# Attention's results stored and reloaded by head, and block-diagonal queries copied once per head

## The chip, the cores and the metric

The kernel runs on one core of a Trainium2 chip. Its engines are TensorE (PE, with its weight loads PEld), VectorE (DVE), ScalarE (ACT), GpSimd (POOL) and SyncE (SP, which here issues every DMA). The metric is device time in microseconds (us), the median of several executions.

## The reference

An attention and two feed-forward layers, one behind the other, all in float32:

```python
# q, k, v: (4 batches, 8 heads, 576 positions, 64)
scores = (q @ k^T) / sqrt(64)
scores = where(pos_i // 64 >= pos_j // 64, scores, -1e9)   # causal by blocks of 64
attn = exp(scores - max);  attn = attn / (sum(attn) + 1e-9)
x = (attn @ v) as (2304 tokens, 512)
h = x @ w_in;  x = (h * clip(h + 3, 0, 6) / 6) @ w_out       # w_in 512x2048, w_out 2048x512
h = x @ w_in2; x = (h * tanh(log1p(exp(h)))) @ w_out2
```

## The kernel before

**Attention** handles 16 pairs of heads, p0 to p15 (4 batches, 4 pairs in each). A value is split in a high and a low part, so that a product takes three matmuls. Queries and keys of a pair come in as `q` and `k` (128 partitions: 64 of each head, 576 positions), and POOL splits them into `qs` and `ks` (`split`, L443 for the high part, L303 for the low one). A pair has three rounds of scores: AC and D, in which each head has its own rows of PE (L526), and BE, in which both heads share a matmul (L495): its stationary operand is block-diagonal, with head 0's queries in one corner, head 1's in the other, and zeros beside them. For p0 POOL copies them into these tiles; for the other pairs DMAs do it, in `last_queries`: four DMAs of 32 KB into `qb` and two into `qe`. The exponentials (ACT, tiles `p..`) are transposed on PE (L555), split again into `z`, and multiplied by the values (L619) into one bank `o`. That is copied out to `x` and stored to DRAM as `x1d[pair of the batch, part, head and dim, token]`, with four DMAs of 64 rows a pair (`attn_v`); the two parts are the 64 upper and 64 lower rows of `x`, which are added later. The reciprocals of the sums go to `rsd` with three DMAs (`sums`).

**First layer.** Tokens run in blocks j (512 columns, the last 256) of four tiles k. `tokens1(j, k)` loads the two parts into `xr` and `xs` (128 rows each), the reciprocals into `xn` (two loads of 64 rows), adds (L934) and scales (L938) on POOL or DVE, and splits the result into the seven `X` tiles (ACT the high part, L303 the low one). `xr` has two buffers, `xs` and `xn` one. PE then runs `h` and `y` (L792 to L794) over 16 slices of weights, which are loaded as `raw` (512 KB each) and rebuilt by ACT, POOL and DVE. **Second layer:** the same with fewer products by sums of blocks; its weights are prepared during the first (`unit2`).

**What sets the order.** Nothing is ordered by hand: `Schedule` takes each operation with its engine, its estimated cost and the names it reads and writes, and writes one sequence per engine. An engine then runs its sequence strictly in order, and a DMA at the head of SP's sequence that waits for its data holds all that stand behind it. The sequence of PE mixes the end of attention with the start of the first layer: the first `h` matmuls stand among the last L619.

Of the kernel before, what the change touches and what calls it, by code (L numbers as in the profile page):

```python
# [10 lines left out]
F32R = mybir.dt.float32r  # L11
# [7 lines left out]
P = 128  # L19
# [210 lines left out]
def f32(ap):  # L230
    return ap.bitcast(F32)
# [7 lines left out]
def fused_kernel(ctx: ExitStack, tc: tile.TileContext, qT, kT, vv, w1, w2, outT):  # L239
# [80 lines left out]
    for n in range(2):  # L320
        for t in "qk":
            at[t, n] = aq.tile([P, S], F32, tag=t, name=f"{t}{n}")
            at[t + "s", n] = aq.tile([P, 2, S], F32R, tag=t + "s", name=f"{t}s{n}")
        at["qb", n] = aq.tile([P, 2, 2, P], F32R, tag="qb", name=f"qb{n}")
        at["qe", n] = aq.tile([P, 2, P], F32R, tag="qe", name=f"qe{n}")
        at["s", n] = ps_s.tile([P, 1024], F32, tag="s", name=f"s{n}")
        at["v", n] = a2.tile([P, 5, P], F32, tag="v", name=f"v{n}")
        at["vb", n] = ap.tile([P, 5, 2, 2, 64], F32R, tag=f"vh{n}", name=f"vh{n}")
        at["z", n] = ap.tile([P, 2, 2, 5 * ZC], F32R, tag=f"t{n}", name=f"z{n}")
        at["su", n] = sm.tile([P, NB], F32, tag="su", name=f"su{n}", bufs=2)  # L330
        at["rs", n] = sm.tile([NB, P], F32, tag="rs", name=f"rs{n}", bufs=2)
        for h in range(2):
            at["x", h, n] = a2.tile([P, S], F32, tag=f"x{h}", name=f"x{h}_{n}")
# [9 lines left out]
    for u in ("AC", "D", "B"):  # L343
# [9 lines left out]
    EARLY_TILES = (  # L353
        [(t, n, j) for t in "qk" for n in range(2) for j in range(2)]
        + [(t, n, i, j) for t in ("qs", "ks") for n in range(2) for i in range(2) for j in range(2)]
        + [("qb", n, j, i) for n in range(2) for j in range(2) for i in range(3)] + [("mask",), ("ones",), ("hold",)]
        + [("s", n) for n in range(2)])
    LATE_TILES = (
        [("v", n) for n in range(2)] + [("vb", n, t) for n in range(2) for t in range(2)]
# [48 lines left out]

    def last_queries(p):
        n = p % 2  # L410
        if p == 0:
            for j in range(2):
                r = slice(64 * j, 64 * j + 64)
                by = lambda t: t.rearrange("p t (n d) -> p t n d", d=64)
                for i, w, dst, src in (
                        (1, 256, at["qb", 0][r, :, :, r], by(at["qs", 0][r, :, P:2 * P])),
                        (0, 128, at["qe", 0][r, :, r], at["qs", 0][r, :, 512:576])):
                    plan.add(
                        one("POOL", "POOL_ONE", w), [("qs", 0, t, 1 - i) for t in range(2)],
                        [("qb", 0, j, m) for m in range(i, 2 * i + 1)],  # L420
                        lambda e, dst=dst, src=src: nc.gpsimd.tensor_scalar(
                            dst, f32(src), 1.0, 1.0, op0=ALU.mult, op1=ALU.mult), after=hold)
            return
        for j in range(2):
            r = slice(64 * j, 64 * j + 64)
            for t in range(2):
                dma(160, [("qs", n, t, 0)], [("qb", n, j, 1 + t)], f32(at["qb", n][r, t, :, r]),
                    f32(at["qs", n][r, t, P:2 * P]).rearrange("p (n d) -> p n d", d=64), land=LAND)
            dma(160, [("qs", n, t, 1) for t in range(2)], [("qb", n, j, 0)],
                f32(at["qe", n][r, :, r]), f32(at["qs", n][r, :, 512:576]), land=LAND)  # L430

    def split(p, t):
        n = p % 2
# [33 lines left out]
    def scores(g):  # L467
# [19 lines left out]

        products = ((0, 0), (0, 1), (1, 0))
        if u == "BE":
            stationary = at["qe", n], at["qb", n][:, :, 0], at["qb", n][:, :, 1]  # L490

            def run(e):
                for k, (x, y) in enumerate(products):
                    for i, a, z, o in BOTH:
                        nc.tensor.matmul(  # L495
                            sc[:, a:z], stationary[i][:, x, :], ks[:, y, a - o:z - o], start=k == 0 and a in (0, 512),
                            stop=k == 2, skip_group_check=True)

            matmuls(
                3 * sum(cost("S", z - a) for _, a, z, _ in BOTH),  # L500
                [("qb", n, j, i) for j in range(2) for i in range(3)] + half("ks", (0, 1)), [("s", g % 2)], run)
            todo = (
                (0, 0, 192, at["p", "B"][:, 0, 0:192], ("p", "B", 0), 7),
                (1, 192, 576, at["p", "E"][:, 0:S], ("p", "E"), 6),
                (2, 768, 256, at["p", "B"][:, 1, :], ("p", "B", 1), 8))
            for c, a, w, *_ in todo:
                maxima(c, sc[:, a:a + w], nm[c][:, 0:1])
            for c, a, w, dst, name, col in todo:
                exps(c, 0, w, a, dst, name, col)
            return  # L510
# [3 lines left out]
        def run(e):  # L514
            for h in range(2):
                r = slice(64 * h, 64 * h + 64)
                out = wide[:, h, groups[0][2] - 128:groups[-1][1] + groups[-1][2]]
                out = out.rearrange("p (g n) -> p g n", n=P)[:, :, 64:P]
                nc.tensor.matmul(
                    out, at["mask"][r], at["ones"][r, 0:64 * len(groups)].rearrange("p (g n) -> p g n", n=64),  # L520
                    start=True, stop=False, skip_group_check=True)
            for k, (x, y) in enumerate(products):
                for i, a, w in groups:
                    for h in range(2):
                        r = slice(64 * h, 64 * h + 64)
                        nc.tensor.matmul(  # L526
                            wide[:, h, a:a + w], qs[r, x, 128 * i:128 * i + 128], ks[r, y, 0:w],
                            start=False, stop=k == 2, skip_group_check=True)

        ns = sum(3 * cost("R", w) for _, _, w in groups) + (90 if u == "AC" else 60)  # L530
# [66 lines left out]
    def attn_v(p, r, h):  # L597
# [41 lines left out]
        plan.add(  # L639
            one("DVE", "DVE_PSUM", w) if h else one("ACT", "ACT_PSUM", w), [("o",)], [("x", h, n, r)], evacuate)  # L640
        if r == 1:
            for t in range(2):
                dma(144, [("x", h, n, i) for i in range(2)], [("x1d", hp, t, b, h)],
                    x1d[hp, t, 64 * h:64 * h + 64, b * S:(b + 1) * S], x[64 * t:64 * t + 64, 0:S])

    def sums(p):
        b, hp = pairs[p]
# [7 lines left out]
            one("DVE", "DVE_PSUM", NB), [("t", k)], cols, lambda e: nc.vector.reciprocal(su, nine))  # L655
        matmuls(cost("T", P), cols, [("t", k)], lambda e: nc.tensor.transpose(tp[0:NB, 1, :], su, ident))
        copy(P, [("t", k)], [("rs", n)], rs, tp[0:NB, 1, :], psum=True)
        for h in range(2):
            dma(60, [("rs", n)], [("rsd", hp, b, h)],
                rsd[hp, h, b * S:b * S + 384].rearrange("(i q) -> i q", q=P), rs[3 * h:3 * h + 3, :])  # L660
        dma(160, [("rs", n)], [("rsd", hp, b, 2)],
            rsd[hp, :, b * S + 384:(b + 1) * S].rearrange("h (n q) -> n h q", q=64),
            rs[6:9, :].rearrange("n (h q) -> n h q", h=2))

# [35 lines left out]
    for n in range(2):  # L700
        for j in range(2):
            r, c = slice(64 * j, 64 * j + 64), slice(64 - 64 * j, P - 64 * j)
            memset(one("POOL", "MEMSET", 256), [("qb", n, j, i) for i in (1, 2)], f32(at["qb", n][r, :, :, c]))
            memset(one("POOL", "MEMSET", 128), [("qb", n, j, 0)], f32(at["qe", n][r, :, c]))
    memset(one("POOL", "MEMSET", 64), [("p", "zero")], at["p", "B"][:, 0, 192:256])
    memset(one("DVE", "MEMSET", 128), [("mask",)], at["mask"])
    for j in range(2):
# [213 lines left out]
    def tokens1(j, k):  # L921
        t0, w = BLOCKS[j]
        raw, low, rs = (buf[t][:, :w] for t in (("xr", k % 2), ("xs", 0), ("xn", 0)))
        r, l, s = ("xr", k % 2), ("xs", 0), ("xn", 0)
        from_ = range(t0 // S, (t0 + w - 1) // S + 1)
        made = [[("x1d", k, t, i, h) for i in from_ for h in range(2)] for t in range(2)]
        land = 7000 if j == 0 else 2500
        dma(w // 2, made[0], [r], raw, x1d[k, 0, :, t0:t0 + w], land=land)
        dma(w // 2, made[1], [l], low, x1d[k, 1, :, t0:t0 + w], land=land)
        for h in range(2):  # L930
            dma(w // 4, [("rsd", k, i, n) for i in from_ for n in range(3)], [("xn", 0, h)] + ([s] if h == 0 else []), rs[64 * h:64 * h + 64],
                rsd[k, h:h + 1, t0:t0 + w].to_broadcast([64, w]), land=land)
# [12 lines left out]

# [379 lines left out]
```

## Time and profile before

| | us |
|---|---|
| median of three runs (lowest, highest) | 935.86 (935.72, 936.88) |
| profiled execution, its own time | 936.84 |
| span that its trace covers | 934.9 |

In the trace's times (from the span's start) attention runs until about 172, the first layer until about 530, the second to the end. In a row of a timeline the first number is the start, the second how long the row's instructions took together, and the bracket says how long the engine was idle before and what ended it; "s" is the bank of scores, and "SPq" the queue in which SP issues DMAs.

### The profile page before, as it was taken

The page shows a single profiled execution, that of the slowest core. Times are in us where ns is not written, and L with a number is a line of the kernel's source. Part 1 is how long each engine was busy: PE and PEld are TensorE (multiplying, and loading weights), DVE is VectorE, ACT ScalarE, POOL GpSimd, SP SyncE. Part 2 cuts the span into 40 slices and gives each one's busy share as a digit, 9 for nine tenths or more (in the row PEclk, how much of TensorE's full clock was granted, in tenths as well). Part 3 has the DMA queues.
Part 4 walks back from the last instruction along what each step waited for, and adds up shares of the span by engine and source line. Part 5 has one row for each costly group of instructions (what it writes and reads, how often), then busy time and mean ns, then how long its engine had stood idle before and what let it go on. Part 6 is the DMA issues. An engine that isn't in the chain of part 4 may idle for free.

```text
span 934.9 us, 16090 instructions
## 1 busy us (share of the span) xinstructions
PE 916.5 (98%) x5328; PEld 837.3 (90%) x5328; DVE 613.3 (66%) x1082; ACT 522.8 (56%) x1207; POOL 610.7 (65%) x636
## 2 busy tenths in 40 slices
PE   7999999899999999999999999999999999999998
PEld 6888888788888888888888899999999999999998
DVE  5899987678946675576222253665697866866657
ACT  6899998667664456454322353644565445644452
POOL 7869778678886549555300031777789777976775
PEclk9999999899999999999999999999999999999999
DMA  5777677689189899888200028767779877796752
GB/s 170 196 200 210 184 222 215 190 274 359 53 281 291 314 290 299 294 294 276 74 1 0 30 89 321 243 226 260 263 274 313 279 263 257 249 318 236 268 211 91
DMA packets 102115, 207.52 MB, mean 222 GB/s; under 512 B 23344, under 2 KB 41360, under 8 KB 102032
## 3 DMA queue, kind: packets, MB, share of 16 engines
q1 hardware_dynamic: 102032, 206.49, 66.9%
q8 instruction: 42, 0.69, 0.3%
q14 instruction: 41, 0.34, 0.1%
HBM read 155.19 MB, written 48.31 MB: 218 GB/s over the span
## 4 chain that ended last, share of the span: by engine, by line
PE 88%; DVE 3%; POOL 3%; ACT 2%; DMA 2%; issue 1%; SPq 1%; DVEq 0%; POOLq 0%; ACTq 0%
PE y L792 13%; PE y L793 13%; PE y L794 13%; PE h L794 10%; PE h L793 10%; PE h L792 10%; PE o L619 4%; PE t L555 3%; PE r L794 3%; PE r L792 3%; PE r L793 3%; PE s L495 2%; PE s L526 2%; DMA qe<-qs 1%; SPq L290 1%
## 5 line engine op out<-in xcount | busy, mean ns | idle before, releaser
L793 PE MATMUL h<-X,wh 128*128 128x512 f32 (+1 forms) x320 | 118.4, 370 | 3.6 <-POOL X L303 3.6
L792 PE MATMUL h<-X,wh 128*128 128x512 f32 (+1 forms) x320 | 118.8, 371 | 0.0
L794 PE MATMUL h<-X,wl 128*128 128x512 f32 (+1 forms) x320 | 118.4, 370 | 0.2 <-DVE wl L846 0.2
L793 PE MATMUL y<-gl,wh 128*128 128x512 f32 (+1 forms) x320 | 117.7, 368 | 0.0
L792 PE MATMUL y<-gh,wh 128*128 128x512 f32 (+1 forms) x320 | 117.7, 368 | 0.0
L794 PE MATMUL y<-gh,wl 128*128 128x512 f32 (+1 forms) x320 | 117.7, 368 | 0.0
L792 PE MATMUL y<-X,wh 128*128 128x384 f32 x336 | 112.5, 335 | 0.9 <-ACT xs L297 0.5
L793 PE MATMUL y<-X,wh 128*128 128x384 f32 x336 | 112.4, 335 | 0.0
L794 PE MATMUL y<-X,wl 128*128 128x384 f32 x336 | 112.3, 334 | 0.0
L303 POOL TENSOR_TENSOR X<-xr,X 128x384 fp32r<-128x384 f32 (+2 forms) x37 | 41.3, 1119 | 103.2 <-ACT X L297 103.1
L899 DVE SCALAR_TENSOR_TENSOR h<-e,h 128x512 f32<-128x512 f32 (+1 forms) x64 | 40.1, 626 | 86.8 <-ACT e L297 86.8
L1134 DVE TENSOR_TENSOR sgh<-y,sgh 128x384 f32<-128x384 f32 x129 | 69.6, 555 | 32.5 <-PE y L794 32.5
L297 ACT ACTIVATE e<-h 128x512 f32<-128x512 f32 (+1 forms) x80 | 44.1, 551 | 71.7 <-PE h L794 71.6
L303 POOL TENSOR_TENSOR X<-e,X 128x384 fp32r<-128x384 f32 x69 | 70.9, 1029 | 11.9 <-ACT X L297 10.0
L793 PEld LDWEIGHTS h<-X,wh 128*128 128x128 f32 x320 | 60.7, 190 | 13.7 <-POOL X L303 3.9
L303 DVE TENSOR_TENSOR z<-t,z 128x512 fp32r<-128x512 f32 (+1 forms) x112 | 67.3, 629 | 7.7 <-ACT z L297 6.5
L480 DVE TENSOR_REDUCE nm<-s 128x2 f32<-128x768 f32 (+2 forms) x96 | 62.4, 678 | 13.0 <-PE s L495 4.3
L794 PEld LDWEIGHTS h<-X,wl 128*128 128x128 f32 x320 | 60.6, 189 | 10.7 <-DVE wl L846 0.6
L792 PEld LDWEIGHTS h<-X,wh 128*128 128x128 f32 x320 | 60.6, 190 | 10.1 <-ACT r L297 0.3
L794 PEld LDWEIGHTS y<-gh,wl 128*128 128x128 f32 x320 | 60.4, 189 | 10.1
L792 PEld LDWEIGHTS y<-gh,wh 128*128 128x128 f32 x320 | 60.3, 188 | 9.9
L793 PEld LDWEIGHTS y<-gl,wh 128*128 128x128 f32 x320 | 60.3, 188 | 9.8
(185 smaller groups left out, 2562.8 us busy)
## 6 DMA issues: line engine op xcount, KB each, us to landing
raw<-w SPq DMA_DIRECT2D x64, 512.0 KB
wh<-w2d SPq DMA_DIRECT2D x48, 512.0 KB
wl<-w2d SPq DMA_DIRECT2D x48, 512.0 KB
wh<-w2d SPq DMA_DIRECT2D x48, 384.0 KB
wl<-w2d SPq DMA_DIRECT2D x48, 384.0 KB
x1d<-x SPq DMA_DIRECT2D x64, 144.0 KB
w2d<-Sh SPq DMA_DIRECT2D x32, 256.0 KB
w2d<-S SPq DMA_DIRECT2D x32, 256.0 KB
```

The lines of the kernel that those rows point to most:

```text
L297: nc.scalar.activation(d, s, func, **kw)
L303: engines, reads, writes, lambda e: ENG[e].tensor_sub(*real(dst, a, b)), **kw)
L480: lambda e: nc.vector.tensor_reduce(to, view, axis=AX.X, op=ALU.max, negate=True))
L495: nc.tensor.matmul(sc[:, a:z], stationary[i][:, x, :], ks[:, y, a - o:z - o], start=k == 0 and a in (0, 512), stop=k == 2, skip_group_chec ...
L526: nc.tensor.matmul(wide[:, h, a:a + w], qs[r, x, 128 * i:128 * i + 128], ks[r, y, 0:w], start=False, stop=k == 2, skip_group_check=True)
L555: nc.tensor.transpose(tp[:, c, :], x, ident)
L619: nc.tensor.matmul(out, vb[:, c, h].rearrange("p t d -> p (t d)"), mov, start=k == 0, stop=k == len(todo) - 1, skip_group_check=True)
L792: nc.tensor.matmul(b, wh, xh, start=start and k == 0, stop=False, skip_group_check=True)
L793: nc.tensor.matmul(b, wh, xl, start=False, stop=False, skip_group_check=True)
L794: nc.tensor.matmul(b, wl, xh, start=False, stop=last, skip_group_check=True)
L899: nc.vector.scalar_tensor_tensor(g, e, 6.0, h, op0=ALU.min, op1=ALU.mult)
L1134: nc.vector.tensor_add(dst, src, old)
```

## The change

- `x1d` is laid out by head: `[pair, head, part and dim, token]`. One DMA of 128 rows stores a head (288 KB); before it took two of 64 rows.
- `rsd` gets two DMAs a pair and not three.
- `tokens1` loads `xr` and `xs` by head: four loads of 64 rows a tile, where there were two of 128. The two loads of `xn` stay.
- The host puts the queries' blocks of 64 in another order (`QUERIES`), so that the three blocks of round BE stand at equal distances of 192 columns. `qe` goes into `qb`, and a pair's six copies become two, one per head (64 rows, six runs of 64 columns, 96 KB); each waits for the high and the low part of all columns.
- The matmuls and their shapes stay as they were.

```diff
+QUERIES = (2, 0, 1, 3, 4, 5, 8, 6, 7)
+QUERY_AT = {0: 64, 2: 256, 3: 448}
...
     def last_queries(p):
...
-            for t in range(2):
-                dma(160, [("qs", n, t, 0)], [("qb", n, j, 1 + t)], f32(at["qb", n][r, t, :, r]),
-                    f32(at["qs", n][r, t, P:2 * P]).rearrange("p (n d) -> p n d", d=64), land=LAND)
-            dma(160, [("qs", n, t, 1) for t in range(2)], [("qb", n, j, 0)],
-                f32(at["qe", n][r, :, r]), f32(at["qs", n][r, :, 512:576]), land=LAND)
+                dma(230, [("qs", n, t, i) for t in range(2) for i in range(2)],
+                    [("qb", n, j, i) for i in range(2)],
+                    f32(dst.rearrange("p t n d -> p (t n) d")[:, :, r]),
+                    f32(src.rearrange("p t (n d) -> p (t n) d", d=192)[:, :, 0:64]), land=LAND)
...
         if r == 1:
-            for t in range(2):
-                dma(144, [("x", h, n, i) for i in range(2)], [("x1d", hp, t, b, h)],
-                    x1d[hp, t, 64 * h:64 * h + 64, b * S:(b + 1) * S], x[64 * t:64 * t + 64, 0:S])
+            dma(90, [("x", h, n, i) for i in range(2)], [("x1d", hp, b, h)],
+                x1d[hp, h, :, b * S:(b + 1) * S], x[:, 0:S])
...
-        for h in range(2):
-            dma(60, [("rs", n)], [("rsd", hp, b, h)],
-                rsd[hp, h, b * S:b * S + 384].rearrange("(i q) -> i q", q=P), rs[3 * h:3 * h + 3, :])
-        dma(160, [("rs", n)], [("rsd", hp, b, 2)],
+        dma(90, [("rs", n)], [("rsd", hp, b, 0)],
+            rsd[hp, :, b * S:b * S + 384].rearrange("h (i q) -> h i q", q=P), rs[0:6, :])
+        dma(160, [("rs", n)], [("rsd", hp, b, 1)],
...
     def tokens1(j, k):
...
-        dma(w // 2, made[0], [r], raw, x1d[k, 0, :, t0:t0 + w], land=land)
-        dma(w // 2, made[1], [l], low, x1d[k, 1, :, t0:t0 + w], land=land)
+        for n, (dst, to) in enumerate(((r, raw), (l, low))):
+            for h, rows in enumerate(heads):
+                dma(w // 3, made[h], [dst + (h,)], to[rows], x1d[k, h, 64 * n:64 * n + 64, t0:t0 + w], land=land)
...
-        "qT": dmajor(q),
+        "qT": dmajor(q.reshape(B, H, NB, 64, D)[:, :, list(QUERIES)]),
```

The costs given to the planner change too, so it writes other sequences for SP and POOL. PE's stays the same but for one transpose (L656) that moves ahead of three matmuls; DVE's stays the same until after the last pair, and ACT's but for two neighbours that change places. Three places follow.

SP in the middle of attention, where the copies into `qb1` for p13 are issued (a number behind a name is a buffer). Before:

```order
L290 DMA xn_173<-rsd_85 64x512
L290 DMA qb1_130<-qs1_127 64x2x64 x2
L290 DMA xn_173<-rsd_85 64x512
L290 DMA raw2_1_1963<-w1 128x1024
L290 DMA k1_128<-kT 128x576
L290 DMA qb1_130<-qs1_127 64x2x64
L290 DMA qe1_131<-qs1_127 64x2x64
L290 DMA qb1_130<-qs1_127 64x2x64
L290 DMA qe1_131<-qs1_127 64x2x64
L290 DMA x1d_84<-x0_0_124 64x576 x2
L290 DMA x1d_84<-x1_0_125 64x576 x2
```

and of the changed kernel:

```order
L292 DMA x1d_84<-x1_1_137 128x576
L292 DMA rsd_85<-rs0_122 3x2x64
L292 DMA rsd_85<-rs0_122 2x3x128
L292 DMA v1_131<-vv 128x640
L292 DMA qb1_129<-qs1_126 64x6x64 x2
L292 DMA q1_125<-qT 128x576
L292 DMA raw3_0_1909<-w1 128x1024
L292 DMA x1d_84<-x0_0_123 128x576
```

The six copies, of which four stood behind a 512 KB load and the load of `k1`, are two, and they stand right behind `v1`, ahead of the loads of `q1` and of weights.

SP at the end of attention, where the loads for block 1 (`xr0`, `xs`, `xn` of its first tile) stand among the stores of p13 (`x0_1`, `x1_1`) and p14 (`x0_0`, `x1_0`). Before:

```order
L290 DMA x1d_84<-x0_1_138 64x576 x2
L290 DMA xr0_164<-x1d_84 128x512
L290 DMA rsd_85<-rs0_123 3x2x64
L290 DMA x1d_84<-x1_1_139 64x576 x2
L290 DMA rsd_85<-rs0_123 3x128 x2
L290 DMA xs_172<-x1d_84 128x512
L290 DMA xn_173<-rsd_85 64x512 x2
L290 DMA x1d_84<-x0_0_124 64x576 x2
L290 DMA xs_172<-x1d_84 128x512
L290 DMA rsd_85<-rs1_137 3x2x64
L290 DMA x1d_84<-x1_0_125 64x576 x2
```

and of the changed kernel:

```order
L292 DMA xs_170<-x1d_84 64x512 x2
L292 DMA x1d_84<-x0_1_136 128x576
L292 DMA xn_171<-rsd_85 64x512 x2
L292 DMA rsd_85<-rs0_122 3x2x64
L292 DMA rsd_85<-rs0_122 2x3x128
L292 DMA x1d_84<-x1_1_137 128x576
L292 DMA xr0_162<-x1d_84 64x512 x2
L292 DMA xs_170<-x1d_84 64x512 x2
L292 DMA x1d_84<-x0_0_123 128x576
L292 DMA xn_171<-rsd_85 64x512 x2
L292 DMA rsd_85<-rs1_135 3x2x64
```

The load of `xs` moves from behind p13's stores and sums to ahead of them; `xr0` moves from ahead of p13's second store to behind it.

POOL at the end of attention (`pE` is p15's copy that its last transpose waits for; X3_1 is the low part of block 0's last tile). Before:

```order
L303 TENSOR_TENSOR X2_1_179<-xr0_164,X2_0_178 128x512
L806 TENSOR_SCALAR q0_165<-raw3_0_2128 128x512
L464 TENSOR_SCALAR vh1_134<-v1_133 128x10x64
L303 TENSOR_TENSOR vh1_134<-v1_133,vh1_134 128x10x64
L934 TENSOR_TENSOR xr1_167<-xr1_167,xs_172 128x512
L938 TENSOR_TENSOR xr1_167<-xr1_167,xn_173 128x512
L806 TENSOR_SCALAR q1_168<-raw3_1_2263 128x512
L576 TENSOR_SCALAR pE_159<-pE_159 128x64
L934 TENSOR_TENSOR xr0_164<-xr0_164,xs_172 128x512
L938 TENSOR_TENSOR xr0_164<-xr0_164,xn_173 128x512
L303 TENSOR_TENSOR X3_1_181<-xr1_167,X3_0_180 128x512
L806 TENSOR_SCALAR val0_161<-raw0_160 128x512
```

and of the changed kernel:

```order
L937 TENSOR_TENSOR xr1_165<-xr1_165,xn_171 128x512
L305 TENSOR_TENSOR X2_1_177<-xr0_162,X2_0_176 128x512
L462 TENSOR_SCALAR vh1_132<-v1_131 128x10x64
L305 TENSOR_TENSOR vh1_132<-v1_131,vh1_132 128x10x64
L801 TENSOR_SCALAR val1_161<-raw2_1_1777 128x512
L801 TENSOR_SCALAR q0_163<-raw3_0_1909 128x512
L801 TENSOR_SCALAR q1_166<-raw3_1_2051 128x512
L933 TENSOR_TENSOR xr0_162<-xr0_162,xs_170 128x512
L574 TENSOR_SCALAR pE_157<-pE_157 128x64
L937 TENSOR_TENSOR xr0_162<-xr0_162,xn_171 128x512
L305 TENSOR_TENSOR X3_1_179<-xr1_165,X3_0_178 128x512
L801 TENSOR_SCALAR val0_159<-raw0_158 128x512
```

L934 and L938 for block 0's last tile (`xr1`) move ahead of the values of p15 (`vh1`); X3_1 still stands behind L934 and L938 of block 1's first tile (`xr0`), in the changed kernel's lines L933 and L937. In the changed kernel's POOL sequence L937 for block 1's second tile comes ahead of the first `gl0`, and X5_1 takes its old place behind `val1`; on SP the weights `raw5_0` and on stand behind the first load of `xr1` for block 1's last tile, which waits for X5_1, and the first 512 KB of the second layer's weights no longer stand ahead of them.

## Rows read from the trace of the kernel before

**Rows 1.** Windows from one pair's round BE to the next; columns: span, PE busy (count), PEclk, DMA share, GB/s.

```profile
122.56:133.45 10.89, 10.02 (x87) 1.00 0.71 196
133.45:144.48 11.03, 10.01 (x90) 1.00 0.76 209
144.48:156.62 12.14, 11.57 (x88) 0.86 0.80 221
156.62:166.38 9.76, 9.76 (x89) 1.00 0.73 210
```

**Rows 2.** Timeline of PE, rounds BE of p11 and p13.

```profile
123.78 0.51 PE L495 MATMUL s<-ks,qe 128*128 128x320 f32 x2 [0.87 <-DMA qe<-qs]
...
144.38 0.33 PE L555 MATMUL t<-ident,pE 128*128 128x128 f32 x1 [1.02 <-DMA qe<-qs]
...
145.37 0.53 PE L495 MATMUL s<-ks,qe 128*128 128x320 f32 x2 [0.57 <-DMA qe<-qs]
```

**Rows 3.** Timeline of POOL before p13's round BE.

```profile
132.25 1.42 POOL L303 TENSOR_TENSOR qs<-q,qs 128x576 fp32r<-128x576 f32 x1
...
137.06 0.68 POOL L440 TENSOR_SCALAR q<-q 128x576 f32<-128x576 f32 x1 [3.39 <-DMA q<-qT]
...
144.08 0.24 POOL L576 TENSOR_SCALAR pE<-pE 128x64 f32<-128x64 f32 x1
```

**Rows 4.** Timeline of SP's DMA issues, the copies for p13.

```profile
136.26 1.31 SPq L290 DMA_DIRECT2D qb<-qs  x2
...
142.14 0.60 SPq L290 DMA_DIRECT2D qe<-qs  x1
```

**Rows 5.** SP's issues by group from 20 to 172 us; ns of one: least/median/most.

```profile
L290 SPq DMA_DIRECT2D qb<-qs x54: 591/618/1178, 21.1 to 161.8; - x54
L290 SPq DMA_DIRECT2D x1d<-x x54: 445/549/1564, 27.2 to 169.6; - x54
L290 SPq DMA_DIRECT2D rsd<-rs x42: 257/306/697, 19.9 to 171.8; - x42
L290 SPq DMA_DIRECT2D qe<-qs x28: 591/605/1013, 21.7 to 162.4; - x28
...
L290 SPq DMA_DIRECT2D xn<-rsd x8: 468/546/603, 25.3 to 167.3; - x8
L290 SPq DMA_DIRECT2D xr<-x1d x5: 425/430/1399, 38.8 to 170.3; - x5
```

**Rows 6.** Timeline of PE, the first matmuls of block 0's last tile.

```profile
176.95 0.45 PE L792 MATMUL h<-X,wh 128*128 128x512 f32 x1
180.97 0.79 PE L793 MATMUL h<-X,wh 128*128 128x512 f32 x1 [3.58 <-POOL X L303]
```

**Rows 7.** Timelines of POOL, SP and ACT ahead of that matmul.

```profile
169.41 1.28 POOL L934 TENSOR_TENSOR xr<-xr,xs 128x512 f32<-128x512 f32 x1 [0.27 <-DMA xs<-x1d]
...
177.03 1.27 POOL L934 TENSOR_TENSOR xr<-xr,xs 128x512 f32<-128x512 f32 x1 [4.13 <-DMA xs<-x1d]
...
179.65 1.26 POOL L303 TENSOR_TENSOR X<-xr,X 128x512 fp32r<-128x512 f32 x1
...
174.19 0.34 SPq L290 DMA_DIRECT2D xs<-x1d  x1
...
173.70 0.61 ACT L297 ACTIVATE X<-xr 128x512 fp32r<-128x512 f32 x1
```

**Rows 8.** Windows: behind that stall, and all that follows; columns as in the page's engines.

```profile
181.00:187.00 6.00, 6.00 (x20) 5.42 (x21) 2.22 (x4) 1.65 (x4) 3.05 (x3) 0.51 0.57 163
...
207.00:935.00 728.00, 723.16 (x3838) 665.12 (x3838) 448.31 (x784) 351.88 (x698) 448.94 (x450) 1.00 0.66 227
```

**Rows 9.** Timelines of POOL, SP and PE where slice 5's weights come in.

```profile
191.84 1.32 POOL L938 TENSOR_TENSOR xr<-xr,xn 128x512 f32<-128x512 f32 x1
...
194.52 20.43 SPq L290 DMA_DIRECT2D raw<-w  x20
...
207.15 0.50 PE L794 MATMUL h<-X,wl 128*128 128x512 f32 x1 [0.15 <-DVE wl L846]
```

More of the change, by code (lines that the diff above doesn't have):

```diff
@@ L323, in fused_kernel @@
             at[t + "s", n] = aq.tile([P, 2, S], F32R, tag=t + "s", name=f"{t}s{n}")
-        at["qb", n] = aq.tile([P, 2, 2, P], F32R, tag="qb", name=f"qb{n}")
-        at["qe", n] = aq.tile([P, 2, P], F32R, tag="qe", name=f"qe{n}")
+        at["qb", n] = aq.tile([P, 2, 3, P], F32R, tag="qb", name=f"qb{n}")
         at["s", n] = ps_s.tile([P, 1024], F32, tag="s", name=f"s{n}")
@@ L355, in fused_kernel @@
         + [(t, n, i, j) for t in ("qs", "ks") for n in range(2) for i in range(2) for j in range(2)]
-        + [("qb", n, j, i) for n in range(2) for j in range(2) for i in range(3)] + [("mask",), ("ones",), ("hold",)]
+        + [("qb", n, j, i) for n in range(2) for j in range(2) for i in range(2)] + [("mask",), ("ones",), ("hold",)]
         + [("s", n) for n in range(2)])
@@ L410, in last_queries @@
         n = p % 2
[L411 to L423, printed above, removed]
         for j in range(2):
             r = slice(64 * j, 64 * j + 64)
-            for t in range(2):
-                dma(160, [("qs", n, t, 0)], [("qb", n, j, 1 + t)], f32(at["qb", n][r, t, :, r]),
-                    f32(at["qs", n][r, t, P:2 * P]).rearrange("p (n d) -> p n d", d=64), land=LAND)
-            dma(160, [("qs", n, t, 1) for t in range(2)], [("qb", n, j, 0)],
-                f32(at["qe", n][r, :, r]), f32(at["qs", n][r, :, 512:576]), land=LAND)
+            src, dst = at["qs", n][r], at["qb", n][r]
+            if p == 0:
+                for i, w, m, x in (
+                        (0, 256, dst[:, :, 0:2, r],
+                         src[:, :, HALVES[0]].rearrange("p t (n d) -> p t n d", d=192)[:, :, :, 0:64]),
+                        (1, 128, dst[:, :, 2, r], src[:, :, 384:448])):
+                    plan.add(
+                        one("POOL", "POOL_ONE", w), [("qs", 0, t, i) for t in range(2)],
+                        [("qb", 0, j, i)], lambda e, m=m, x=x: nc.gpsimd.tensor_scalar(
+                            m, f32(x), 1.0, 1.0, op0=ALU.mult, op1=ALU.mult), after=hold)
+            else:
+                dma(230, [("qs", n, t, i) for t in range(2) for i in range(2)],
+                    [("qb", n, j, i) for i in range(2)],
+                    f32(dst.rearrange("p t n d -> p (t n) d")[:, :, r]),
+                    f32(src.rearrange("p t (n d) -> p (t n) d", d=192)[:, :, 0:64]), land=LAND)
     def split(p, t):
@@ L489, in scores @@
         if u == "BE":
-            stationary = at["qe", n], at["qb", n][:, :, 0], at["qb", n][:, :, 1]
+            stationary = [at["qb", n][:, :, i] for i in (2, 0, 1)]
             def run(e):
@@ L500, in scores @@
                 3 * sum(cost("S", z - a) for _, a, z, _ in BOTH),
-                [("qb", n, j, i) for j in range(2) for i in range(3)] + half("ks", (0, 1)), [("s", g % 2)], run)
+                [("qb", n, j, i) for j in range(2) for i in range(2)] + half("ks", (0, 1)), [("s", g % 2)], run)
             todo = (
@@ L526, in run @@
                         nc.tensor.matmul(
-                            wide[:, h, a:a + w], qs[r, x, 128 * i:128 * i + 128], ks[r, y, 0:w],
+                            wide[:, h, a:a + w], qs[r, x, QUERY_AT[i]:QUERY_AT[i] + P], ks[r, y, 0:w],
                             start=False, stop=k == 2, skip_group_check=True)
@@ L702, in fused_kernel @@
             r, c = slice(64 * j, 64 * j + 64), slice(64 - 64 * j, P - 64 * j)
-            memset(one("POOL", "MEMSET", 256), [("qb", n, j, i) for i in (1, 2)], f32(at["qb", n][r, :, :, c]))
-            memset(one("POOL", "MEMSET", 128), [("qb", n, j, 0)], f32(at["qe", n][r, :, c]))
+            memset(one("POOL", "MEMSET", 384), [("qb", n, j, i) for i in range(2)], f32(at["qb", n][r, :, :, c]))
     memset(one("POOL", "MEMSET", 64), [("p", "zero")], at["p", "B"][:, 0, 192:256])
@@ L925, in tokens1 @@
         from_ = range(t0 // S, (t0 + w - 1) // S + 1)
-        made = [[("x1d", k, t, i, h) for i in from_ for h in range(2)] for t in range(2)]
+        made = [[("x1d", k, i, h) for i in from_] for h in range(2)]
+        heads = [slice(64 * h, 64 * h + 64) for h in range(2)]
         land = 7000 if j == 0 else 2500
-        dma(w // 2, made[0], [r], raw, x1d[k, 0, :, t0:t0 + w], land=land)
-        dma(w // 2, made[1], [l], low, x1d[k, 1, :, t0:t0 + w], land=land)
-        for h in range(2):
-            dma(w // 4, [("rsd", k, i, n) for i in from_ for n in range(3)], [("xn", 0, h)] + ([s] if h == 0 else []), rs[64 * h:64 * h + 64],
+        rr = [r, r + (0,), r + (1,)]
+        for n, (dst, to) in enumerate(((r, raw), (l, low))):
+            for h, rows in enumerate(heads):
+                dma(w // 3, made[h], [dst + (h,)], to[rows], x1d[k, h, 64 * n:64 * n + 64, t0:t0 + w], land=land)
+        for h, rows in enumerate(heads):
+            dma(w // 4, [("rsd", k, i, n) for i in from_ for n in range(2)], [s + (h,)], rs[rows],
                 rsd[k, h:h + 1, t0:t0 + w].to_broadcast([64, w]), land=land)
         plan.add(
-            one("POOL", "POOL", w), [r, l], [r], lambda e: nc.gpsimd.tensor_add(raw, raw, low))
+            one("POOL", "POOL", w), [*rr, l, l + (0,), l + (1,)], rr,
+            lambda e: nc.gpsimd.tensor_add(raw, raw, low))
         of = either(w) if j == 1 else one("POOL", "POOL", w)
         plan.add(
-            of, [r, s, ("xn", 0, 0), ("xn", 0, 1)], [r],
+            of, [*rr, s, s + (0,), s + (1,)], rr,
             lambda e: ENG[e].tensor_mul(raw, raw, rs))
@@ L940, in tokens1 @@
         at = [("X", X(j, k), h) for h in range(2)]
-        copy(w, [r], [at[0]], hi, raw)
-        sub(of, [r, at[0]], [at[1]], lo, raw, f32(hi))
+        copy(w, rr, [at[0]], hi, raw)
+        sub(of, rr + [at[0]], [at[1]], lo, raw, f32(hi))
     def unit2(u):
```

## The prediction

> **What bounds the kernel now.** I read the windows first. A window from one pair's round BE to the next is one pair, and the last of the four shown holds 9.76 us of span and 9.76 us of PE: that is what a pair costs when nothing is late. The three ahead of it, from p11 to p14, take 10.89, 11.03 and 12.14 us, and PE waits in each [rows 1]. From 207 us to the end PE is busy 723.16 of 728.00 us at full clock [rows 8]: DMA, DVE, ACT and POOL all have room there, so whatever the change does behind 207 can hardly win anything. The gain, if there is one, lies in attention and at the seam to the first layer.
>
> Next, who is late there. Ahead of the long pairs PE waits for `qe` (0.87 us for p11, 0.57 for p13), and for p13 also for the transpose of p15's copy `pE` (1.02 us, whose named releaser is a DMA) [rows 2]. But the data of these copies are old: POOL ends the low part of p13's `qs` at 132.25 + 1.42 = 133.67 [rows 3], while SP issues two of the `qb` copies at 136.26 and the last `qe` copy at 142.14, 8.5 us later [rows 4]. PE gets it at 145.37, 3.23 us after that issue [rows 2]. So SP's queue is late, not POOL and not the transfer. The medians of SP's issues say why [rows 5]: a pair's stores and copies are 4 × 0.618 (`qb`) + 2 × 0.605 (`qe`) + 4 × 0.549 (`x1d`) + 3 × 0.306 (`rsd`) = 6.80 us of issuing out of 9.76, and the loads of q, k, v, weights and tokens come on top, each in strict order, some waiting at the head. The same queue makes the load of `q` late: POOL idles 3.39 us for it at 137.06, and its copy of `pE`, behind that in POOL's sequence, ends only at 144.08 + 0.24 [rows 3], just ahead of PE's 1.02 us wait.
>
> At the seam PE stands still for 3.58 us ahead of 180.97 for X3_1, the low part of block 0's last tile [rows 6]. X3_1's own input was ready: ACT had its high part by 173.70 + 0.61. It stands on POOL behind L934 and L938 of block 1's first tile, and that L934 waited 4.13 us for `xs` [rows 7]. The buffer `xs` had been free since 169.41 + 1.28 = 170.69, but SP issued the load at 174.19, 3.50 us late, because p13's stores and sums stand ahead of it; it landed 2.84 us after its issue. Behind the stall the granted clock is 0.51 for the 6 us from 181 to 187, the lower of the two levels (1.2 of 2.4 GHz), with PE busy all the time [rows 8].
>
> **The change, part by part.** PE's and DVE's sequences in attention stay, so the matmuls cost what they did; the terms are waits.
>
> *Queries.* SP's six copies a pair, 4 × 0.618 + 2 × 0.605 = 3.68 us, become two. No row has a copy of six runs in 64 rows. From below it costs what two runs cost, 0.618 (two: 1.24); from above it grows with the runs, 3 × 0.618 = 1.85 (two: 3.71, so nothing saved). *Results.* Four stores of 64 rows (2.20 us) become two of 128. The nearest rows are 0.430 (`xr`, 128 rows of 512) and 0.549 (`x1d`, 64 rows) [rows 5], so 0.86 to 1.10. *Sums.* Three become two: 0.92 to 0.61. Together 6.80 becomes 2.71 to 5.42 us: SP is freed of 1.4 to 4.1 us a pair. I take the lower half of the cost, since 128 rows at 0.430 against 64 at 0.549 show that issue does not grow with the bytes.
>
> Against it stand the loads by head. A tile had 2 × 0.430 + 2 × 0.546 = 1.95 us of issue; with four loads of 64 rows at `xn`'s 0.546 it has 3.28, so 1.33 more, for four tiles or so in attention (the five `xr` of rows 5). That is 5 us over the last 60 us against at least 6 × 1.4 = 8.4 us saved there. The other tiles are loaded behind 207, where PE has no wait for them to lengthen.
>
> *Is the new copy in time?* It waits for all of `qs`, that is until 133.67 for p13 (before, the copies of the high part could go earlier, but the last one counted). PE wants it at 145.37 − 0.57 = 144.80 at the earliest, and 144.80 − 0.57 − 1.02 ≈ 143.2 with the two waits gone. So 9.5 us are there. Two copies issued back to back (1.24) and landing as the last did (3.23) need 4.5; so the waits on `qe` go. The same 192 KB went through the same queue before, only in six parts. What is late next is ACT or DVE, which carry PE's other waits, and the fourth window shows a pair with no such wait.
>
> *The pairs' term.* (10.89 − 9.76) + (11.03 − 9.76) + (12.14 − 9.76) = 1.13 + 1.27 + 2.38 = 4.78 us [rows 1]. Of the 2.38 I count all, its clock of 0.86 too, since the lower clock comes behind waits of PE.
>
> *The seam's terms.* In the new order `xs` for block 1's first tile is ahead of p13's stores. PE arrives at the L793 of X3 at 176.95 + 0.45 − 4.78 ≈ 172.6. For X3_1 to be ready, the load of `xs` must be issued when the buffer falls free (170.69 − 4.78 ≈ 165.9) and land 2.84 us later, at 168.8; then L934 (1.27), L938 (1.32, its row of 191.84 [rows 9]) and X3_1 (1.26) end at 172.65. ACT's high part, at 173.70 + 0.61 − 4.78 ≈ 169.5, is no hindrance. So with no delay at all the load by its old duration just meets PE, with nothing in hand; a microsecond of delay would be a wait of a microsecond, though `xs` can fall free earlier still, since POOL's work on `q` is no longer held up. I count the stall of 3.58 as gone. With it goes the slow clock: 6.00 us at 0.51 would be 6 × 0.51 = 3.06 at full clock, so 2.94.
>
> *Slice 5.* PE's wait of 0.15 at 207.15 shows slice 5's weights just in time [rows 9]. Behind the change these `raw` loads stand behind a load that waits for X5_1, which sits where L938 sat at 191.84; both move forward with PE, and 512 KB of other weights leave from ahead of them. I count zero, and up to 1 us of new wait within the next allowance.
>
> **Sum.** 4.78 + 3.58 + 2.94 = 11.30, less an allowance of 0.5 for small new waits (the size of the smallest wait in rows 2): 10.8. The profiled execution's own time is 936.84, so 926.0; the median of the runs is 0.98 under that execution, so the forecast is 925.1.
>
> **A rule against it.** Rows 5 show only that a load of 64 rows costs SP more issue than one of 128; how long two halves take to land no row here shows, as `x1d` was always loaded with 128 rows. The Trainium skill, "SBUF — State Buffer", section "Can I just issue two DMAs to hit both halves?", advises one 128-partition transfer, and "Door 1: The DMA port swizzle (why [64,N] ≈ [32,N])" has 64 partitions reach half of the ports, 196 against 328 GB/s at 1 MiB. My estimate by that page for a 256 KB part is 1.34 against 0.80 us, about 0.5 us more if the halves go one behind the other: by it the sum would be 10.3 and not 10.8, and at the seam more if several loads queue.
>
> **The rivals.**
> *Loads by head are late at the seam.* Eight loads for a tile's two parts and sums stand where four stood, and if the second half of `xs` lands a whole 2.84 us behind the first, X3_1 comes at 175.4, PE stalls some 2.8 us and the slow clock stays. Against it: SP has 8 us more room ahead of it. For it: nothing in hand. Then little more than the pairs' 4.78 is won: 936.84 − 4.78 = 932.1 own, 931.1 by the median.
> *The one copy lands too late (slower).* It cannot start before all of `qs`, and it has six runs a row. If landing grew with the runs, 3 × 3.23 = 9.7, and issue 3.71, `qb` would come 13.4 us after `qs`, 2.6 us behind the 10.8 from 133.67 to the 144.48 at which the window begins. For 15 pairs that is 39 us: 936.84 − 10.8 + 39, about 965. It decides from where a pair's new wait times 15 eats the gain, 10.8 / 15 = 0.72 us, so from 11.5 us between split and landing. Against it: the bytes are the same, and the six copies together took no such time.
> *No change.* The waits on `qe` were covered by others: `pE` or ACT's exponentials come just as late, and in the new POOL order L934, which waits for `xs`, stands ahead of `pE`. Each long pair keeps its length and the seam gets only what it loses: within 2 us of 935.9.
>
> **How the numbers follow.** The forecast gets 0.64 (923 to 928), late loads at the seam 0.20 (929 to 932.5), no change 0.07, the late copy 0.07, better than 923 0.02. A measurement here can tell about 0.2%, 1.9 us. Faster by more than that: 0.64 + 0.20 + 0.02 = 0.86; within it 0.07; slower 0.07. The range from 923.0 to 931.8 holds the forecast and most of the late loads, 8 in 10.
>
> **What would show it.** Right: the copies into `qb` issued within a microsecond or so of the low part of `qs`, no PE wait for `qb`, POOL not idle for `q`, the windows of p11 to p14 at 9.76; at the seam L793 of X3 without a wait and a granted clock of 1.00 on to 207. Wrong: SP held at the head by a load whose buffer is not free, so that copies are late again; an issue of `qb` near 1.85 us; `xs` landing well over 2.84 us after its issue; or a new wait at X5_1 or slice 5, where loads now stand behind others.

## The result, and the profile after

The changed kernel takes 925.11 us (median of 4 runs, 924.80 to 927.39) against 935.79 us of the kernel before in the same comparison: a ratio of 0.9893, 95% interval 0.9871 to 0.9916. The profiled execution took 925.06 us, with a span of 922.8.

Windows of the changed kernel from one round BE to the next, p11 to p15, then up to the place where the stall ended before, to 207 us, and the rest. Columns as in [rows 1] and [rows 8]: span; busy time of PE, PEld, DVE, ACT and POOL; PEclk; DMA share; GB/s.

```profile
122.45:132.24 9.79, 9.79 (x86) 9.12 (x87) 8.59 (x17) 9.26 (x30) 8.13 (x9) 1.00 0.83 279
132.24:142.01 9.77, 9.77 (x90) 9.10 (x88) 8.81 (x17) 9.54 (x31) 8.51 (x10) 1.00 0.82 247
142.01:151.78 9.77, 9.77 (x90) 9.10 (x88) 8.81 (x17) 9.55 (x31) 7.86 (x9) 1.00 0.56 163
151.78:161.54 9.76, 9.76 (x89) 9.09 (x87) 8.80 (x17) 9.53 (x31) 9.37 (x10) 1.00 0.38 121
161.54:181.00 19.46, 19.40 (x128) 17.16 (x127) 16.67 (x31) 16.79 (x41) 14.11 (x15) 1.00 0.54 154
181.00:207.00 26.00, 26.00 (x116) 21.35 (x115) 21.71 (x34) 17.58 (x32) 21.69 (x23) 1.00 0.92 353
207.00:922.00 715.00, 711.35 (x3789) 655.62 (x3787) 429.91 (x761) 343.73 (x682) 442.67 (x443) 1.00 0.66 225
```

The four pairs, 43.82 us in [rows 1], take 39.09 us, each with PE busy all the time. The clock is 1.00 throughout. Before, the same two stretches behind p15's round BE read:

```profile
166.38:181.00 14.62, 10.98 (x82) 9.87 (x80) 10.40 (x20) 10.60 (x29) 9.91 (x11) 0.97 0.69 189
181.00:207.00 26.00, 26.00 (x110) 21.61 (x110) 16.06 (x26) 14.47 (x26) 18.74 (x17) 0.89 0.73 231
```

What PE still waits for in the changed kernel, up to 240 us (total, times, longest): no DMA, no `pE` and no X.

```profile
PE s L493 <- ACT pAC L483: 2.3, 5, 0.5
PE t L553 <- ACT pAC L483: 1.7, 2, 1.4
PE t L553 <- DVE z L305: 1.6, 2, 0.9
PE t L387 <- POOL ident masks.py:199: 1.4, 1, 1.4
PE s L524 <- POOL ks L305: 0.7, 1, 0.7
PE t L553 <- ACT rs L299: 0.2, 1, 0.2
```

SP's issues from 20 to 172 us, the counterpart of [rows 5] (ns: least/median/most):

```profile
L292 SPq DMA_DIRECT2D rsd<-rs x31: 260/643/704, 19.8 to 169.9; - x31
L292 SPq DMA_DIRECT2D x1d<-x x30: 320/342/578, 27.1 to 170.6; - x30
L292 SPq DMA_DIRECT2D qb<-qs x28: 612/628/1344, 20.6 to 146.6; - x28
...
L292 SPq DMA_DIRECT2D xr<-x1d x12: 445/504/599, 32.4 to 171.6; - x12
```

And the places of [rows 3], [rows 4] and [rows 7]: SP's copies for p14, the two loads of `xs` for block 0's last tile (140.88 and, not shown, 142.07) and for block 1's first (153.70), and the load of `xr` for the latter (161.43). Then POOL's split that releases those copies, its `q`, its L933 for the two tiles, and X3_1 (the row at 169.10).

```profile
136.14 1.32 SPq L292 DMA_DIRECT2D qb<-qs  x2
...
140.88 0.50 SPq L292 DMA_DIRECT2D xs<-x1d  x1
...
153.70 1.12 SPq L292 DMA_DIRECT2D xs<-x1d  x2
...
161.43 1.11 SPq L292 DMA_DIRECT2D xr<-x1d  x2
```

```profile
134.69 1.43 POOL L305 TENSOR_TENSOR qs<-q,qs 128x576 fp32r<-128x576 f32 x1
...
138.36 0.67 POOL L438 TENSOR_SCALAR q<-q 128x576 f32<-128x576 f32 x1
...
152.38 1.30 POOL L933 TENSOR_TENSOR xr<-xr,xs 128x512 f32<-128x512 f32 x1
...
165.11 1.29 POOL L933 TENSOR_TENSOR xr<-xr,xs 128x512 f32<-128x512 f32 x1 [1.02 <-PE o L617]
...
169.10 1.28 POOL L305 TENSOR_TENSOR X<-xr,X 128x512 fp32r<-128x512 f32 x1 [1.26 <-ACT X L299]
```

The copies are issued at 136.14, at the end of the low part of `qs` (134.69 + 1.43 = 136.12), where p13's last one stood 8.5 us behind it in [rows 4]; SP now waits for the data, not the data for SP. POOL's `q` follows its work without idle time, where it had waited 3.39 us. L933 of block 1's first tile does not wait for `xs`, which was issued at 153.70, 11 us ahead of it. The releaser named in its row is PE, but L933 reads only `xr` and `xs`, so its 1.02 us are for the load of `xr`, issued 3.7 us ahead at 161.43.

### The profile page after: what moved, and what is told of

Its sections match the earlier page's. It is cut to its first block, busy times and chain, and to the rows that moved or that the text cites. A ratio compares the mean times of both kernels' runs of the same rounds, so it can differ in the third digit from the quotient of the medians.

```text
span 922.8 us, 15996 instructions
## 1 busy us (share of the span) xinstructions
PE 910.4 (99%) x5328; PEld 833.0 (90%) x5328; DVE 606.8 (66%) x1078; ACT 523.5 (57%) x1207; POOL 614.6 (67%) x636
## 4 chain that ended last, share of the span: by engine, by line
PE 92%; DVE 3%; ACT 2%; DMA 1%; issue 1%; POOL 0%; SPq 0%; DVEq 0%; ACTq 0%
PE y L787 13%; PE y L788 13%; PE y L789 13%; PE h L787 11%; PE h L789 11%; PE h L788 11%; PE o L617 4%; PE t L553 4%; PE s L493 3%; PE r L788 3%; PE r L787 3%; PE r L789 3%; PE s L524 2%; ACT pAC L483 1%; DVE z L305 1%; DMA q<-qT 1%
## 5 line engine op out<-in xcount | busy, mean ns | idle before, releaser
L789 PEld LDWEIGHTS h<-X,wl 128*128 128x128 f32 x320 | 60.4, 189 | 10.1
```

The costliest lines, as they stand in the source:

```text
L789: nc.tensor.matmul(b, wl, xh, start=False, stop=last, skip_group_check=True)
```

## The experiments

Two theories and some side ones were set against each other. **Theory Q**: SP's issue time was nearly used up in attention, so loads and copies came late, whichever stood last. **Theory O**: the planner's new order, not the number or length of the issues, made the difference. The side theories have their letters in the expectations.

**One part alone: queries.** The changed kernel with the old stores, sums and token loads.

```diff
-            dma(90, [("x", h, n, i) for i in range(2)], [("x1d", hp, b, h)],
-                x1d[hp, h, :, b * S:(b + 1) * S], x[:, 0:S])
+            for t in range(2):
+                dma(144, [("x", h, n, i) for i in range(2)], [("x1d", hp, t, b, h)],
+                    x1d[hp, t, 64 * h:64 * h + 64, b * S:(b + 1) * S], x[64 * t:64 * t + 64, 0:S])
...
```

> Changed kernel with the old stores by part (four of 64 rows), the old three stores of sums and the old token loads of 128 rows; the new order of queries and the two copies a pair stay. Theory Q (SP's issue time makes everything late; the copies are its largest piece): the copies free 3.68 - 1.26 = 2.4 of the 3.9 us that the whole change frees a pair, the windows of p11 to p14 come down to 9.8 us, and most of the pairs' 4.8 us is won: 925 to 931 us. Theory O (what counts is the place of copies and loads in SP's sequence, which the planner chose anew): about 925 too if the copies come early, but then e2 gives nothing. Theory S (the loads of tokens by head, which start earlier, are what takes the stall at the seam away): the seam's 6.5 us stay, about 931.

925.58 us, ratio 0.9897 (0.9882 to 0.9911): not to be told from the whole change. Its windows of the pairs are those of the changed kernel:

```profile
122.56:132.35 9.79, 9.79 (x86) 9.12 (x87) 8.59 (x17) 9.27 (x30) 8.15 (x9) 1.00 0.86 279
132.35:142.12 9.77, 9.77 (x90) 9.10 (x88) 8.81 (x17) 9.55 (x31) 8.52 (x10) 1.00 0.72 220
```

Theory S falls: the stall at the seam is gone too, with tokens loaded as before.

**The other part alone: results, sums and token loads.** Six copies a pair as before.

```diff
-            for t in range(2):
-                dma(144, [("x", h, n, i) for i in range(2)], [("x1d", hp, t, b, h)],
-                    x1d[hp, t, 64 * h:64 * h + 64, b * S:(b + 1) * S], x[64 * t:64 * t + 64, 0:S])
+            dma(90, [("x", h, n, i) for i in range(2)], [("x1d", hp, b, h)],
+                x1d[hp, h, :, b * S:(b + 1) * S], x[:, 0:S])
...
```

> Kernel before with stores of a head as one DMA, the sums in two and the token loads by head; queries and their six copies a pair as before. Theory Q: only 1.5 us of SP's issue is freed a pair (four x1d of 0.549 become two of 0.342), and loads by head take some of it back, so the copies stay late in part: 927 to 933 us. Theory O: the copies stand where they stood, so the waits on them stay: the pairs' 4.8 us are not won, 931 or more. Theory S: the seam's stall goes, 6.5 us won, about 929, with PE's waits for qe left in the pairs.

928.01 us, ratio 0.9921 (0.9906 to 0.9936). PE waits for no `qe` any more, although there are as many copies of it as before; what stays are 0.5 us for `qb`, once, and `pE`:

```profile
PE t L555 <- POOL pE L576: 1.5, 2, 1.1
```

So one part wins 10.4 us and the other 7.9, and both together 10.7: the gains don't add. That speaks for a limit that either part lifts, against prices per DMA.

**Issue time put back, order kept.** Behind a pair's second copy SP issues two, four or six DMAs that nobody needs; every other sequence is that of the changed kernel.

```diff
             d, s = real(dst, src)
             nc.sync.dma_start(d, s)
+            for x in more:
+                d, s = real(*x)
+                nc.sync.dma_start(d, s)
...
+                    more=[(idle[p, i], f32(src[:, :, 16 * i:16 * i + 16])) for i in range(IDLE)] if j else [])
```

> As the run with six idle DMAs a pair, with two. SP's issue time a pair rises by 2 x 0.604 = 1.2 us to about 7.0 of a pair's 9.76. Theory Q (a queue: nothing happens until SP is nearly full): within 2 us of 925. Rival (each issue costs its share, 24.4 us / 6 = 4 us per idle DMA a pair): 933.

> The same with four idle DMAs a pair: 2.4 us more, about 8.2 us a pair, which is what the kernel before has. Theory Q: queries' loads begin to be late, 927 to 940 us, about where the kernel before is. Rival (in proportion): 941.

> Changed kernel, every engine's sequence the same, but behind a pair's second copy SP issues six more DMAs (64 rows of two runs of 16 columns, 8 KB each, to a place in DRAM that nobody reads). SP's issue time a pair is what it was before (about 3.6 us more) with little data. Theory Q: queries, stores and tokens are late again, POOL waits for q, PE for pE or qb, and the time goes back towards 935 (over 929). Theory O: the sequence is the new one, so the time stays within 2 us of 925.

Two: 925.29 us (0.9884, 0.9866 to 0.9902). Four: 933.63 (0.9975, 0.9959 to 0.9991). Six: 949.49 (1.0148, 1.0125 to 1.0171). Two cost nothing, the next two 8 us, the last two 16. In-proportion rivals and theory O fall; only the size with six was expected too small. What POOL waits for with six, and what PE waits for:

```profile
POOL q L445 <- DMA q<-qT: 19.4, 8, 4.5
...
POOL xr L940 <- DMA xs<-x1d: 7.0, 2, 4.0
```

```profile
PE o L624 <- ACT x L642: 7.4, 5, 3.0
PE t L560 <- POOL pE L581: 2.6, 2, 1.9
```

`q` is late as in the kernel before, and beside `pE` there is a new wait: ACT can't copy out to `x`, since its store is late as well, and PE's values wait for ACT:

```profile
ACT x L642 <- DMA x1d<-x: 10.0, 5, 3.7
```

Could it be the DMA engines that the idle DMAs fill, and not SP? From 20 to 140 us their share is 0.79 in the changed kernel, 0.81 with two, 0.75 with four and 0.68 with six idle DMAs a pair: it falls where time is lost. But the price isn't issue time alone. From 20 to 172 us SP also waits at the head of its queue for earlier DMAs to land, 13 us in all with four and 9 with six, against 5 in the kernel before and 3 in the changed one.

**Order changed, issues kept.** The kernel before, with the planner told that some DMAs are wanted 6 us earlier: the copies, the loads of `q`, or both.

```diff
             need[i] = min((need[k] for k in after[i]), default=t + 4000) - cost
+            if i in self.first:
+                need[i] -= 6000
```

> Kernel before, all DMAs as they were, but the planner counts the copies of queries as wanted 6 us earlier, so that SP takes them ahead of loads and stores. Theory Q: SP has as much to issue, so the wait moves to q, v or the tokens: within 2 us of 935.9, or slower. Theory O: the waits on qe go and the pairs' 4.8 us are won: 931 or less.

> Kernel before, all DMAs as they were, but the planner counts the loads of q as wanted 6 us earlier. POOL's idle time for q (3.39 us in rows 3) is the link by which SP's lateness came to pE and PE. Theory Q: SP has as much to issue, so something else is late in its place: within 2 us of 935.9 or slower. Rival O2 (it is the place of q's load alone): 931 or less.

> Kernel before with both the loads of q and the copies of queries counted as wanted 6 us earlier, so that stores, sums and tokens wait instead. Theory Q in its strict form (SP is short of time for all of it): the stores of x1d or the tokens are late, PE waits for x buffers or at the seam, within 3 us of 935.9. Rival O (order could have won it without fewer issues): the pairs' 4.8 us are won, 931 or less.

936.63 us (1.0012, 0.9998 to 1.0025), 937.58 (1.0015, 0.9997 to 1.0033) and 940.22 (1.0041, 1.0023 to 1.0060): none is faster. The wait goes where SP's lateness is pushed. With the copies first, `q` is late and through it `pE`, for POOL and for PE:

```profile
POOL q L442 <- DMA q<-qT: 19.3, 5, 6.5
```

```profile
PE t L557 <- POOL pE L578: 4.7, 2, 3.0
```

With `q` first, it is `qe` again, and X at the seam:

```profile
PE h L797 <- POOL X L305: 3.9, 1, 3.9
PE s L499 <- DMA qe<-qs: 2.4, 3, 1.4
```

With both first, `q` was late all the same (POOL waited 20.5 us for it): its load of 126.36, say, stands behind four stores issued from 121.06 and three of sums from 123.58. None of these three orders wins; that no order at all could isn't shown.

Across these runs SP's issuing from 20 to 172 us, summed as count times median over its groups (for the kernel before 54 x 0.618 + 54 x 0.549 + ... = 121 us), stands beside the time:

| run | issuing, us of 152 | share | median, us |
|---|---|---|---|
| changed kernel | 87 | 57% | 925.11 |
| queries only | 97 | 64% | 925.58 |
| two idle DMAs | 106 | 69% | 925.29 |
| results only | 119 | 78% | 928.01 |
| four idle DMAs | 119 | 78% | 933.63 |
| before | 121 | 80% | 935.79 |
| six idle DMAs | 124 | 82% | 949.49 |

Up to 69% the time doesn't move; near 80% it does, and by how much depends on what stands behind the issues (the two at 78%). The three orders stand at 122, 121 and 120 us, about where the kernel before does. The table is rough, since count times median leaves out single long issues: added up one by one, the kernel before has 130 us and that with six idle DMAs 127. So the share tells where the limit is, and not the price. The rest of SP's time goes in waits at the head of its queue.

**The price of a stall at the seam.** The load of `xs` for block 1's first tile comes behind seven copies of itself, one after the other.

```diff
+                    before=[(to[rows], x1d[k, h, 64 * n:64 * n + 64, t0:t0 + w])] * LATE if (j, k, n, h) == (1, 0, 1, 0) else [])
```

> Changed kernel; ahead of the first half of xs for block 1's first tile the same load is issued seven times more, each waiting for the landing of the one before, so that this tile comes some 16 to 20 us later than before; sequences otherwise the same. It prices the stall at the seam. Theory K (a stall of PE there costs itself and a stretch at the lower clock behind it): PE stands still for 2 to 8 us at X3 or near, the granted clock falls behind it, and the time is 925 plus the stall plus about 3. Rival L (only the stall counts, the lower clock is made up for later): 925 plus the stall. Rival N (slack hides it): no stall, 925.

939.54 us, ratio 1.0031 (1.0015 to 1.0046). The stall came, though at p15's `pE`, which stands behind L933 (here L939) on POOL, and not at X3. What POOL waited for is the load of `xr`, which the late `xs` held up in SP's queue until 176.34. SP's, POOL's and PE's timelines, and the windows behind the stall:

```profile
176.34 1.11 SPq L294 DMA_DIRECT2D xr<-x1d  x2
...
180.22 1.26 POOL L939 TENSOR_TENSOR xr<-xr,xs 128x512 f32<-128x512 f32 x1 [15.68 <-DMA xr<-x1d]
...
181.74 0.48 PE L556 MATMUL t<-ident,pE 128*128 128x128 f32 x1 [10.88 <-POOL pE L577]
...
196.26 0.47 PE L790 MATMUL h<-X,wh 128*128 128x512 f32 x1 [0.79 <-ACT r L302]
```

```profile
182.00:184.00 2.00, 2.00 (x6) 1.61 (x6) 1.12 (x3) 1.36 (x3) 2.00 (x2) 0.50 0.51 129
184.00:187.00 3.00, 3.00 (x11) 2.52 (x11) 0.47 (x1) 0.43 (x2) 2.03 (x3) 0.50 0.52 175
187.00:190.00 3.00, 3.00 (x20) 2.52 (x20) 2.22 (x4) 1.65 (x4) 0.00 (x0) 1.00 0.75 222
```

10.88 + 0.79 of waits and (187.00 - 181.74) x 0.5 = 2.6 for the lower clock give 14.3 of the 937.7 - 922.8 = 14.9 us by which the span grew. Theory K holds.

**Token loads whole again.** One DMA of 128 rows for a part, from the layout by head.

```diff
-            for h, rows in enumerate(heads):
-                dma(w // 3, made[h], [dst + (h,)], to[rows], x1d[k, h, 64 * n:64 * n + 64, t0:t0 + w], land=land)
+            dma(w // 2, made[0] + made[1], [dst + (0,), dst + (1,)], to, x1d[k, :, 64 * n:64 * n + 64, t0:t0 + w], land=land)
```

> Changed kernel, but each part of a tile's tokens is loaded by one DMA of 128 rows (256 KB, both heads) in place of two of 64 rows; sequences of PE and of POOL in attention the same. Theory Q: SP issues some 0.5 us less a part and PE waits for no load in either kernel, so the time stays within 1.9 us of the changed kernel's 925.1. Rival (the Trainium skill's page SBUF — State Buffer: halves of 64 rows reach half of the ports): the whole loads land some 0.5 us earlier each by my estimate, which the trace would show, and the first POOL adds of the first layer's tokens wait less; 1 to 2 us faster if any of that is on PE's path.

1015.99 us, ratio 1.0846 (1.0824 to 1.0868): both expectations failed, by 90 us. SP issues one such load at 182.71 and a second some 4 us later (one row, x2), and POOL, idle for 10.90 us, gets what it waits for at 193.84:

```profile
182.71 4.19 SPq L292 DMA_DIRECT2D xr<-x1d  x2
```

```profile
193.84 1.26 POOL L932 TENSOR_TENSOR xr<-xr,xs 128x512 f32<-128x512 f32 x1 [10.90 <-DMA xr<-x1d]
```

From 184 to 193 us SP issues nothing but these loads. The queue's row of that stretch (packets, MB, share of the 16 engines' time):

```profile
q1 hardware_dynamic: 244, 0.46, 13.3%
```

13.3% is close to 2 of 16 (12.5%), and 0.46 MB in 9 us is 51 GB/s, at which 256 KB alone take 5 us, and two loads together twice that. So the transfer is slow, and not its issue: by the sum of the table SP issues for 77 us here, less than in the changed kernel. The source here is `[2 heads, 64, w]`, whose outermost dimension is 2.

**The same loads with another outermost dimension.** `x1d` by part, dim, head and token: a store is still one DMA, and a load has 128 rows at one distance. The rows of `w_in` are put in that order on the host, and the two loads of `xn` are one.

```diff
-    x1d = dpool.tile([KT, 2, P, NT], F32, tag="x1d", name="x1d")
+    x1d = dpool.tile([KT, 2, 64, 2, NT], F32, tag="x1d", name="x1d")
...
+                x1d[k, n, :, :, t0:t0 + w].rearrange("d h t -> (d h) t"), land=land)
```

> Changed kernel with x1d laid out as part, dim, head, token: a head is still stored by one DMA of 128 rows, and a part of a tile is loaded by one DMA of 128 rows whose outermost dimension is 128 and not 2 (rows come as dim and head in turn; the rows of w_in are put in the same order on the host); the reciprocals come in one load, not two. Same loads in number and bytes as the run with whole loads by head, whose loads landed some 10 us after issue. Theory E (there a load with an outermost dimension of 2 is carried by 2 of the 16 DMA engines): the loads land in 2 to 4 us and the time is 924 to 927, no better than the changed kernel, since PE waits for no load in it. Rival W (fewer, larger token loads are bad in themselves, by the buffers that they hold or the order that the planner then makes): over 950 again.

926.39 us, ratio 0.9900 (0.9884 to 0.9917), not to be told from the changed kernel. The loads of `xr` and `xs` are as many and as large as in the run before this one, and POOL shows no wait for them from 20 to 200 us, so the 90 us go with the outermost dimension, which is theory E. The Trainium skill, "DMA: Bandwidth & Descriptors", section "Rules for kernel authors", states it: the slowest dimension of either side sets how many of the 16 engines a DMA uses. The share of 13.3% agrees.

## Why the prediction was right

The time came out at 925.11 where 925.1 was forecast, but that closeness is partly luck: the profiled execution took 925.06 where 926.0 was forecast, and where the kernel before had its median 0.98 us under that execution, which the forecast took over, the changed kernel's is 0.05 above it. The two misses cancel.

*The pairs' term*, 4.78 us: measured 43.82 - 39.09 = 4.73. *The stall*, 3.58: gone, so 3.58. *The clock*, 2.94: (1 - 0.89) x 26 = 2.86 from 181 to 207 (the 0.97 ahead of 181 costs nothing, as PE stands still there). These three make 11.17 of the 936.84 - 925.06 = 11.78 us won. The other 0.6, in waits too small to have a term (the 0.15 of slice 5 [rows 9] is gone too), and the allowance of 0.5 for new waits, which wasn't used, are the 1 us by which the profiled execution came out better than forecast. The late-token experiment shows that a stall does bring the lower clock and both their prices.

*SP's saving.* Of the range 1.4 to 4.1 us a pair, the copy is at its low end: 0.628 against 0.618 to 1.85, so six runs cost the issue of two. The store of 128 rows took 0.342, less than the 0.430 of the low end. The sums were wrong: "Three become two: 0.92 to 0.61" fails, since the merged store takes some 0.66 and the pair about 0.97, nothing saved. With 2 x 0.628, 2 x 0.342 and 0.97, 6.80 becomes 2.91, 3.9 saved.

*The copy's room.* "So 9.5 us are there" subtracts the wait of 0.57 twice: by its own rows it is 10.1. In the changed kernel p13's copies are issued at 126.37 for a round that begins at 142.01, 15.6 us later: POOL, no longer idle for `q`, splits sooner. And the `pE` ahead of p13's round is p12's, not p15's.

*The step that failed in its mechanism* is the slack at the seam. I put the load of `xs` at 165.9 and had X3_1 "just meet PE, with nothing in hand". It was issued at 153.70, and that for block 0's last tile at 140.88, where it had been 166.16; X3_1 was done at 170.38, 2 us ahead of its matmul at 172.42. All tokens came earlier because SP had time for them, not because one load passed p13's stores: the `xs` of block 0's last tile was issued 0.6 us after its buffer fell free (138.99 + 1.30 = 140.29), where before it was 8.8 us (156.12 + 1.28 = 157.40). What X3_1 waited for last was ACT's high part, which the prediction called no hindrance (its row at 169.10, 1.26 us); the 2 us are what is left with that. Of the rival of late loads at the seam, with 0.20, only POOL's 1.02 us for `xr` came, and it cost PE nothing.

*The rule against it.* Two halves let POOL start later than one whole load, by how much isn't settled. The two for `xr` issued from 171.07 let POOL start at 175.23, 4.16 us, where the whole load of the queries-only run, issued at 172.15, let it start at 175.31, 3.16 us: 1.0 us more, 0.55 of it the second issue, and the rest would be near the prediction's estimate of 0.5. But for the tile before it 161.43 to 165.11 stands against 163.58 to 166.81, 0.45 us more, which the second issue covers alone. It costs nothing, as PE doesn't wait for it.

*The rivals.* The late copy doesn't occur. "No change" named the right neighbours, `pE` and ACT: with the copies first it is just what happened, since then `pE` is as late as the copies were. It fails for the change because SP's issues became fewer, not only other, and that is shown from both sides: the new order with the old issue time back in it loses, and none of three orders with the old issues wins. The Trainium skill, "Perfetto Trace Analysis", section "What "DMA-bound" means", lists this bound, the issuing engine's sequencer track filled with DMAs, as one apart from the DMA engines' own. The traces agree: the pairs of [rows 1] lose time at a DMA share of 0.71 to 0.80, and the first two of the changed kernel lose none at 0.83 and 0.82.

## What to carry to other kernels

Add up the issue time of the queue that issues all DMAs and set it against the time of a stage: well below its limit (69% here) another DMA is free, near it (80%) each makes whatever stands last late, and in the three orders tried moving some ahead only moved the wait. Gains from thinning out such a queue don't add; half of the change here was enough. When DMAs are merged, look at the outermost dimension of both sides: two loads became one here, and 90 us were lost.

## What was not expected of the hardware

Loads of 256 KB whose source has 2 as its outermost dimension moved at 51 GB/s on 13.3% of the DMA engines, and one that shared them with a second took 11 us; a load of 128 rows at one distance took 3.2 (172.15 to 175.31, queries only). SP's issue time doesn't follow bytes: a store of 128 rows and 288 KB took 0.342 us, one of 64 rows and 144 KB 0.549, a copy of 64 rows in six runs 0.628, and a store of 3 KB as 2 x 3 x 128 about 0.66.
